# An SSM convolution with a ReLU MLP: the filter loaded in two halves, its tables made in another order and on other engines

## The chip, the core and the metric

The kernel runs on one core of a Trainium2 chip. The core has a matrix engine (TensorE, "PE" in the profile, with its weight loads as "PEld"), a vector engine (VectorE, "DVE"), a scalar engine (ScalarE, "ACT"), a general engine (GpSimd, "POOL") and a queue engine (SyncE, "SP") that here only issues DMA transfers. ACT issues a few as well. Each engine works through its own list in order. Matmuls write to PSUM, and ACT or DVE copy the result to SBUF ("evacuate" it). POOL does not touch PSUM here.

The metric is the time of one execution on the device in microseconds (us), the median over runs.

## The reference

Sequence length S is 2048, width D is 512, the hidden width of the MLP is 1376. All inputs are bf16.

```python
def A(q, k, v, shift_k, ssm_k, ssm_D):
    k_shift = sum over t < 4 of k_pad[:, t:t+S] * shift_k[:, 3 - t]   # short causal filter
    kv = k_shift * v
    y = causal convolution of kv with ssm_k over the places (FFT of length 2S, cut to S)
    y = y + kv * ssm_D
    return q * y

def B(x, w1, w2):
    return relu(x @ w1) @ w2

h   = x + A(layernorm(x), k, v, shift_k, ssm_k, ssm_D)      # x is A_q
out = h + B(layernorm(h), w1, w2)
```

## The kernel before, in words

The long convolution is a transform of length 4096 in two stages, done as matmuls against tables of sines that the kernel makes itself. The order of work is written out by hand: the framework keeps the order of the calls per engine and adds the waits. What sets the order around the change is therefore the list of calls at the end of the function (L476 to L556).

**Tables.** `_turns` (L182) makes whole-number phases on DVE with two operations, a multiply-add and a bitwise mask; `_sin` (L177) turns them into sines on ACT. The first stage's table is `f1f` (128 x 64). It is split into a bf16 high and low part (`f1hi`, `f1lo`, L242 to L244), and `paired` (L253) spreads the two over `f1w` with one memset and eight POOL copies of 32 partitions each. The second stage's table is `tab` (128 x 32 x 4 x 64): slots 0 and 1 come from ACT in four pieces (`sines2`, L272), slots 2 and 3 are their negatives, made by POOL (`negated`, L275). The phases of the pieces with i = 1 are put in two buffers (`tb`, L138) that belong to `kT` before k is loaded there. `inverse_turns` (L291) prepares phases of the inverse tables on POOL.

**Loads.** `load_rows` (L104) brings ssm_k into `kfl`, eight transfers of 256 KB: row groups 0 and 2 on SP's queue, 1 and 3 on ACT's. `wsh` (shift_k) and `drow` (ssm_D) are small transfers on ACT's queue. Then SP's queue brings k, transposed, in four chunks (`load_k`, L140), v in six transfers (`load_v`, L112), the first quarter of x (`load_x0`, L161, into `qn0`), and w1 in four (`load_w1`, L154).

**Stages.** `warm` (L418) issues matmuls whose result is not used. `s1(0)` to `s1(7)` are the first stage for ssm_k (`stage1`, L343; matmuls L350 for ssm_D's term, `drow2`, and L358). Each writes two PSUM tiles, and a string such as "AD" says which engine evacuates which (A is ACT, D is DVE). s1(gb) uses the places 8 gb to 8 gb + 7 of `kfl`. `tap(u, eng)` (L368) is the short filter over k as matmuls against `wdiag`, which `diagonals` (L261) makes on POOL from `wsh`. `second_k(kp, eng)` (L396) is the second stage for ssm_k, 16 calls, each needing slots 0 to 2 of its part of `tab`. `row(q)` (L466, L329) transposes the filtered k and multiplies by v on DVE into `xfl`, the input called "x" of the convolution. Then eight `stage1` calls do x's first stage into `a1x`, 16 `product` calls (L571) do its second stage and the products with the filter's transform, and the inverse follows (L612 on), with the gating, both layer norms and the MLP.

In the products DVE multiplies the one half from PSUM (L580); the other half (L585) is multiplied by POOL for ten of the 16, from an SBUF copy that ACT makes (L579, three buffers), and by DVE for the rest.

PSUM has four tiles (two pools of two, `bank2`, L322), taken in turn. So a matmul group may have to wait until the group four tiles earlier has been evacuated.

**x's layer norm and w1.** `bn_stats`, `moments` (L444) and `norm_rows` (L451) normalise the first quarter of x in place in `qn0`, on DVE but for two small POOL operations. `column_means` (L404) sums w1 over its rows with matmuls, and `center` (L412) subtracts the means from w1 on POOL.

Of the kernel before, what the change touches and what calls it, by code (L numbers as in the profile page):

```python
# [15 lines left out]
P = 128  # L16
# [39 lines left out]
def kernel(  # L56
# [47 lines left out]
    def load_rows(eng, rg):  # L104
        for d in range(2):
            src = bass.AP(tensor=A_ssm_k.tensor, offset=A_ssm_k.offset + S * first_channel(rg, d), ap=[[64, 32], [S, 64], [1, 64]])
            eng.dma_start(out=kfl[32 * rg:32 * rg + 32, :, d, :], in_=src)
# [4 lines left out]
    def load_v(r):  # L112
        for d in range(2) if r % 2 else (0,):
            n = 64 if r % 2 else P
            src = bass.AP(tensor=A_v.tensor, offset=A_v.offset + first_channel(r, d), ap=[[64 * D, 32], [D, 64], [1, n]])
            nc.sync.dma_start(out=vfl[32 * r:32 * r + 32, :, 64 * d:64 * d + n], in_=src)
# [8 lines left out]
    nc.vector.memset(drow2[:], 0.0)  # L125
    nc.scalar.dma_start(out=wsh[:], in_=A_shift_k.rearrange("(r p) j -> p r j", p=P))
    nc.scalar.dma_start(out=drow[0:P:16, :], in_=A_ssm_D.rearrange("(r g) -> r g", g=64))
    load_rows(nc.scalar, 1)
    for rg in (0, 2):
        load_rows(nc.sync, rg)  # L130
# [5 lines left out]


    tb = [chunk(f"tb{b}")[:].rearrange("p c t -> p (c t)").bitcast(I32)[:, 0:1024].rearrange("p (a b) -> p a b", b=64) for b in range(2)]  # L138
# [83 lines left out]
    load_rows(nc.scalar, 3)  # L222
# [5 lines left out]

    def turns2(i, b):
        ta = tb[b] if i else early.tile([P, 16, 64], I32, tag="ta", name="ta", bufs=2)[:]  # L230
        _turns(ta, r2, n2c[:], 8192, o2[:, i, b:b + 1])
        return ta

    ta00 = turns2(0, 0)
    ta01 = turns2(0, 1)
    f1hi = consts.tile([P, 64], BF16, name="f1hi")
    f1lo = consts.tile([P, 64], BF16, name="f1lo")
    f1d = early.tile([P, 64], F32, name="f1d")


    tab = tabp.tile([P, 32, 4, 64], F32R, name="tab")
    nc.vector.tensor_copy(out=f1hi[:], in_=f1f[:])  # L242
    nc.vector.tensor_tensor(out=f1d[:], in0=f1f[:], in1=f1hi[:], op=ALU.subtract)
    nc.vector.tensor_copy(out=f1lo[:], in_=f1d[:])  # L244

    f1w = consts.tile([P, 2, 2, 64], BF16, name="f1w")

    def spikes():
        for rg in range(DC):
            q = slice(32 * rg, 32 * rg + 32)  # L250
            nc.vector.tensor_copy(out=drow2[q, rg % 2, :], in_=drow[q, :])  # L251

    def paired():  # L253
        nc.gpsimd.memset(f1w[:], 0.0)
        for rg in range(DC):
            for i, f in enumerate((f1hi, f1lo)):
                nc.gpsimd.tensor_copy(out=f1w[32 * rg:32 * rg + 32, i, rg % 2, :], in_=f[32 * rg:32 * rg + 32, :])  # L257
# [14 lines left out]
    def sines2(i, b, ta):  # L272
        _sin(tab[:, 16 * i:16 * i + 16, b, :], ta, 8192)

    def negated(i):  # L275
        nc.gpsimd.tensor_single_scalar(out=tab[:, 8 * i:8 * i + 8, 2:4, :], in_=tab[:, 8 * i:8 * i + 8, 0:2, :].bitcast(F32),
                                       scalar=-1.0, op=ALU.mult)
# [173 lines left out]
    def norm_rows(q, out, src):  # L451
        for i in range(4):
            t = 4 * q + i
            nc.vector.tensor_scalar(out=out[:, i, :], in0=src[:, i, :], scalar1=mv1[:, t, 0:1],
                                    scalar2=rstd1[:, t, :], op0=ALU.subtract, op1=ALU.mult)
# [19 lines left out]

    load_k(0)  # L476
    load_k(1)
    spikes()
    sines2(0, 0, ta00)
    ta10 = turns2(1, 0)  # L480
    sines2(0, 1, ta01)
    ta11 = turns2(1, 1)
    diagonals()
    paired()
    negated(0)
    negated(1)
    sines2(1, 0, ta10)
    sines2(1, 1, ta11)
    load_k(2)
    load_k(3)  # L490
    load_v(0)
    load_v(2)
    load_x0()
    load_v(1)
    load_v(3)
    load_w1()
    negated(2)
    negated(3)
    inverse_turns()
    warm(13, lhsT=wdiag[:, 0, 0:2].rearrange("p j g -> p (j g)"))  # L500
# [3 lines left out]
    tap(0, "A")  # L504
    s1(3, "AD")
    s1(4, "AD")
    tap(1, "D")
    s1(5, "AD")
    s1(6, "AD")
    s1(7, "AD")  # L510
    tap(2, "A")
    second_k(0, "A")
    second_k(1, "D")
    second_k(2, "A")
    tap(3, "A")
    second_k(3, "D")
    second_k(4, "A")
    tap(4, "A")
    second_k(5, "D")
    pairs_pool()  # L520
    second_k(6, "A")
    tap(5, "D")
    nc.vector.bn_stats(out=st[:, 0, :], in_=qn0[:, 0, :])
    second_k(7, "A")
    tap(6, "A")
    nc.vector.bn_stats(out=st[:, 1, :], in_=qn0[:, 1, :])
    second_k(8, "A")
    tap(7, "D")
    nc.vector.bn_stats(out=st[:, 2, :], in_=qn0[:, 2, :])
    nc.vector.bn_stats(out=st[:, 3, :], in_=qn0[:, 3, :])  # L530
    moments(mv1, rstd1, 0)
    second_k(9, "A")
    row(0)
    second_k(10, "D")
    norm_rows(0, qn0, qn0)
    second_k(11, "A")
    row(1)
    second_k(12, "A")
    row(2)
    second_k(13, "D")  # L540
    second_k(14, "A")
    row(3)
    second_k(15, "A")
    pl.pop("front")
    a1xp = pl.push("a1xp")
    a1x = a1xp.tile([P, 2, 32, 256], F32R, name="a1x")
    for gb in range(8):
        stage1(lambda g: xfl[:, g // 4, :, :, g % 4], a1x, gb, ("DA", "AD", "AD", "AD", "AA", "AD", "AD", "AD")[gb])
        if gb == 0:
            column_means(0)  # L550
            for n in (0, 1):
                center(n)
        if gb == 2:
            column_means(1)
            for n in (2, 3):
                center(n)  # L556
    pl.pop("xp", "rows")

    late = pl.push("late")
    prod = pl.push("prod")  # L560
# [295 lines left out]
```

## Time and profile before

| | |
|---|---|
| three runs | 203.06, 203.39, 203.69 us; median 203.39 |
| the profiled execution | 203.05 us, of which the span (first to last instruction) is 201.3 us |
| busy in the span | PE 172.1, PEld 109.2, DVE 147.5, ACT 98.0, POOL 90.7 us |
| moved | 15.99 MB in 51,379 packets |
| chain that ended last | PE 67%, DVE 18%, POOL 4%, ACT 4% |

A row of the profile names a source line (L358 is line 358 of the kernel above), an engine, an operation, and `output<-inputs` by the program's names, with partitions x elements. "ACTq" and "SPq" are the issuing of DMA transfers by those engines; such a row's length is the time of the issue, not of the transfer, and the time to landing counts from the start of the issue. In a timeline row the first number is the start in us from the beginning of the span, the second the length; "x31" says that 31 neighbouring instructions are merged, and the bracket at the end gives the idle time before and what ended it. In a group row the numbers after the bar are busy us, mean ns of one, idle us before them and who ended it. In a list of waits the numbers are us in total, times, and the longest.

### The profile page before, as it was taken

What the parts mean: (1) busy time and instruction counts of PE and PEld (TensorE: products, weight loads), DVE (VectorE), ACT (ScalarE), POOL (GpSimd) and SP (SyncE); (2) the same over time, 40 slices, a digit from 0 to 9 for tenths busy, and PEclk for the clock granted to TensorE, in tenths of its full rate; (3) what the DMA queues carried; (4) which work ended last, traced back from release to release, by engine and by line L of the source; (5) the groups of instructions that cost most, each with busy time, mean ns of one, the idle gap of its engine ahead of it and who ended that gap; (6) DMA issues with size and microseconds to landing.
All of it is one profiled execution on the core that took longest, in us unless ns stands there. A gap on an engine that the chain in (4) does not pass through costs nothing.

```text
span 201.3 us, 4078 instructions
## 1 busy us (share of the span) xinstructions
PE 172.1 (86%) x1638; PEld 109.2 (54%) x1643; DVE 147.5 (73%) x259; ACT 98.0 (49%) x112; POOL 90.7 (45%) x108
## 2 busy tenths in 40 slices
PE   0369989899896877778967999999999999999992
PEld 0127866498775666656745654545454444444451
DVE  7957866999557999999999779979977580471142
ACT  0387688924786566522985568102630174026300
POOL 7999983120299699991985720220130011002000
PEclk9999999999999999999999999999999999999999
DMA  8999999960000000005902540312420272120022
GB/s 118 216 233 200 212 205 145 187 146 0 3 3 3 0 5 0 0 3 160 235 22 52 154 129 11 61 37 61 101 47 19 61 83 50 38 54 13 3 54 52
DMA packets 51379, 15.99 MB, mean 79 GB/s; under 512 B 46784, under 2 KB 50208, under 8 KB 51360
## 3 DMA queue, kind: packets, MB, share of 16 engines
q1 hardware_dynamic: 42464, 14.61, 35.8%
q10 hardware_dynamic: 8896, 1.12, 3.6%
q8 instruction: 13, 0.21, 0.4%
q14 instruction: 6, 0.05, 0.1%
HBM read 9.64 MB, written 2.10 MB: 58 GB/s over the span
## 4 chain that ended last, share of the span: by engine, by line
PE 67%; DVE 18%; POOL 4%; ACT 4%; issue 3%; ACTq 2%; DVEq 0%; POOLq 0%
PE m L726 19%; PE m L781 18%; DVE a1x L580 7%; PE ps L358 5%; DVE zs L619 5%; PE ps2k L388 4%; PE u L388 4%; PE pkv L375 3%; PE pst L333 3%; DVE a1k L585 3%; ACT a1x L317 3%; PE pz L646 3%; PE pi L614 2%; PE pz L656 2%; POOL f1w L257 2%
## 5 line engine op out<-in xcount | busy, mean ns | idle before, releaser
L762 ACT ACTIVATE h1T<-m 128x512 bf16<-128x512 f32 (+1 forms) x44 | 25.9, 598 | 43.5 <-PE m L726 43.5
L726 PE MATMUL m<-hT,w 128*128 128x512 bf16 (+1 forms) x176 | 39.0, 379 | 0.2 <-ACT hT L693 0.2
L781 PE MATMUL m<-w,h1T 128*128 128x512 bf16 (+1 forms) x161 | 36.1, 379 | 0.2
L787 DVE SCALAR_TENSOR_TENSOR o<-m,rstd,hp 128x128 bf16<-128x128 f32 (+1 forms) x48 | 15.8, 388 | 25.7 <-PE m L781 24.9
L448 POOL TENSOR_SCALAR rstd<-mv 128x4 f32<-128x4 f32 x8 | 1.8, 231 | 64.4 <-DVE mv L446 64.4
L726 PEld LDWEIGHTS <-w 128*128 128x128 bf16 (+1 forms) x176 | 17.4, 100 | 20.4 <-issue 0.5
L781 PEld LDWEIGHTS <-h1T 128*128 128x128 bf16 (+1 forms) x165 | 16.0, 98 | 19.3 <-issue 0.3
L388 PE MATMUL u<-a1x,tab 64*128 64x256 f32 x256 | 19.7, 291 | 6.4 <-DVE a1k L585 2.4
L585 POOL TENSOR_TENSOR a1k<-usb,a1k 128x1024 fp32r<-128x1024 f32 x10 | 23.7, 2393 | 2.3 <-DVE a1x L580 2.2
L627 ACT CAST a1x<-zs 128x1024 fp32r<-128x1024 f32 (+2 forms) x10 | 17.3, 1730 | 11.1 <-DVE zs L619 11.1
L388 PEld LDWEIGHTS u<-a1x,tab 64*128 64x128 f32 x256 | 16.4, 185 | 9.7 <-DVE a1x L580 4.2
L580 DVE TENSOR_TENSOR a1x<-u,a1k 128x1024 fp32r<-128x1024 f32 x16 | 19.1, 1218 | 2.2 <-PE u L388 2.2
L625 POOL CAST a1x<-zs 128x1024 fp32r<-128x1024 f32 (+1 forms) x8 | 15.7, 1969 | 7.4 <-DVE zs L619 7.4
L619 DVE STREAM_TRANSPOSE zs<-pi 128x1024 f32<-128x1024 f32 x16 | 18.4, 1215 | 0.5 <-PE pi L614 0.5
L414 POOL TENSOR_TENSOR w<-w,wm 128x1376 bf16<-128x1376 bf16 x4 | 11.2, 2844 | 11.3 <-ACT wm L410 11.3
L614 PE MATMUL pi<-a1k,wd 128*128 128x512 f32 x32 | 13.3, 417 | 2.6 <-DVE zs L619 1.5
L579 ACT COPY usb<-u 128x1024 f32<-128x1024 f32 x10 | 10.1, 1016 | 10.3 <-PE u L388 10.3
L317 ACT CAST a1k<-ps2k 128x1024 fp32r<-128x1024 f32 x11 | 11.0, 1027 | 7.1 <-PE ps2k L388 7.0
L614 PE MATMUL pi<-a1x,wd 128*128 128x512 f32 x32 | 12.8, 400 | 0.0
L319 DVE CAST a1k<-ps 128x1024 fp32r<-128x1024 f32 x8 | 9.6, 1222 | 4.4 <-PE ps L358 4.4
L319 DVE CAST a1x<-ps 128x1024 fp32r<-128x1024 f32 x7 | 8.4, 1222 | 5.1 <-PE ps L358 5.1
L421 PE MATMUL warm<-zero,wdiag 128*128 128x512 bf16 x13 | 4.5, 518 | 8.4 <-DVE drow L251 8.4
(116 smaller groups left out, 281.1 us busy)
## 6 DMA issues: line engine op xcount, KB each, us to landing
xall<-in_A_q_dram SPq DMA_DIRECT2D x16, 128.0 KB, 3.3
out_dram<-o SPq DMA_DIRECT2D x62, 32.0 KB, 1.6
w<-in_B_w_dram SPq DMA_DIRECT2D x4, 344.0 KB, 6.1
w<-in_B_w_dram SPq DMA_DIRECT2D x1, 1280.0 KB, 7.7
kfl<-in_A_ssm_k_dram SPq DMA_DIRECT2D x4, 256.0 KB, 5.6
kfl<-in_A_ssm_k_dram ACTq DMA_DIRECT2D x4, 256.0 KB, 6.7
vfl<-in_A_v_dram SPq DMA_DIRECT2D x2, 512.0 KB, 6.7
vfl<-in_A_v_dram SPq DMA_DIRECT2D x4, 256.0 KB, 5.4
```

The lines of the kernel that those rows point to most:

```text
L317: nc.scalar.copy(out=o, in_=i)
L319: nc.vector.tensor_copy(out=o, in_=i)
L388: nc.tensor.matmul(out=ps[:, d, 256 * i:256 * i + 256], lhsT=tab[rw, k1, b:b + 2, :].rearrange("p b k -> p (b k)"), rhs=a_in[rw, c, k1, :] ...
L580: nc.vector.tensor_tensor(out=spot(a1x, kp), in0=u2[:], in1=kk.bitcast(F32), op=ALU.mult)
L585: (nc.gpsimd if pool else nc.vector).tensor_tensor(out=kk, in0=(usb if pool else u1)[:], in1=kk.bitcast(F32), op=ALU.mult)
L614: nc.tensor.matmul(out=ps[:, b, :], lhsT=wd[:, m:m + 2, :].rearrange("p b k -> p (b k)"), rhs=src[:, d, 16 * b:16 * b + 16, c0:c0 + 32], s ...
L619: nc.vector.transpose(out=zs[:], in_=ps[:].rearrange("p b (k c) -> p c (b k)", c=32))
L627: nc.scalar.copy(out=o, in_=i)
L726: nc.tensor.matmul(out=ps1[:fsz].rearrange("p (i t) -> p i t", i=4), lhsT=w1[:, c, fc * P:fc * P + fsz], rhs=hT[sc][:, c // 2, :, c % 2, : ...
L762: nc.scalar.activation(out=h1T[:fsz, fc, :], in_=ps1[:fsz], func=ACT.Relu)
L781: nc.tensor.matmul(out=ps2[:], lhsT=lhsT, rhs=w2[:ksz, fc, :], start=(fc == 0), stop=(fc == NFC - 1))
L787: nc.vector.scalar_tensor_tensor(out=of(o[:], d)[:, a], in0=ps[:, a], scalar=rstd2[:, t, :], in1=pair(hp[sc][:, d, i, :])[:, a], op0=ALU.m ...
```

## The change

- **ssm_k in halves.** `load_rows(part, pairs)` loads places 0 to 31 of each channel block or places 32 to 63, so there are 16 transfers of 128 KB. The first eight come ahead of everything else on both queues. Of the second eight, ACT issues two after the sines of `f1f` and two after the first piece of `tab`. `drow` and `wsh` move to SP's queue, between the halves.
- **f1w by masks.** `paired` and `spikes` become two plus two and two DVE operations on all 128 partitions, with a 0/1 column per row group. The POOL copies, the memset and the split into `f1hi` and `f1lo` go.
- **Second table.** The phases sit in one tile `tt` of two pieces instead of in `kT`'s buffers. DVE makes the pieces with i = 0 early; the multiply-add of i = 1 goes to POOL and its mask to DVE, late, between the taps. `negated` takes one slot at a time, so there are eight of half the size, of which `negated(0, 0)` and `negated(1, 0)` come first.
- **Order.** 24 warm-up matmuls that read only `zero`, instead of 13 that need `wdiag`. All eight s1 come ahead of the first tap. The rows come later among the second_k calls. k, v, x0 and w1 are loaded in the order k, v, x0, w1.
- **w1's means.** `column_means(0)` and its `center` calls move ahead of x's first stage, `column_means(1)` from after its third to after its second call. The layer norm statistics of x's first quarter move behind the rows, and `norm_rows(0)` to POOL.

Second_k and tap evacuations are dealt out anew between ACT and DVE. The diff, with blank lines and unchanged context cut:

```diff
...
     kfl = front.tile([P, 64, 2, 64], BF16, name="kfl")
-    def load_rows(eng, rg):
-        for d in range(2):
-            src = bass.AP(tensor=A_ssm_k.tensor, offset=A_ssm_k.offset + S * first_channel(rg, d), ap=[[64, 32], [S, 64], [1, 64]])
-            eng.dma_start(out=kfl[32 * rg:32 * rg + 32, :, d, :], in_=src)
+    def load_rows(part, pairs=(0, 1)):
+        for pair in pairs:
+            for d in range(2):
+                for eng, rg in ((nc.sync, 2 * pair), (nc.scalar, 2 * pair + 1)):
+                    src = bass.AP(tensor=A_ssm_k.tensor, offset=A_ssm_k.offset + S * (first_channel(rg, d) + 32 * part),
+                                  ap=[[64, 32], [S, 32], [1, 64]])
+                    eng.dma_start(out=kfl[32 * rg:32 * rg + 32, 32 * part:32 * part + 32, d, :], in_=src)
     vfl = front.tile([P, 64, P], BF16, name="vfl")
-    def load_v(r):
-        for d in range(2) if r % 2 else (0,):
-            n = 64 if r % 2 else P
-            src = bass.AP(tensor=A_v.tensor, offset=A_v.offset + first_channel(r, d), ap=[[64 * D, 32], [D, 64], [1, n]])
-            nc.sync.dma_start(out=vfl[32 * r:32 * r + 32, :, 64 * d:64 * d + n], in_=src)
+    def load_v(eng, r, d):
+        n = 64 if r % 2 else P
+        src = bass.AP(tensor=A_v.tensor, offset=A_v.offset + first_channel(r, d), ap=[[64 * D, 32], [D, 64], [1, n]])
+        eng.dma_start(out=vfl[32 * r:32 * r + 32, :, 64 * d:64 * d + n], in_=src)
     zero = consts.tile([P, 512], BF16, name="zero")
     nc.vector.memset(zero[:], 0.0)
...
     nc.vector.memset(drow[:], 0.0)
     drow2 = consts.tile([P, 2, 64], BF16, name="drow2")
-    nc.vector.memset(drow2[:], 0.0)
-    nc.scalar.dma_start(out=wsh[:], in_=A_shift_k.rearrange("(r p) j -> p r j", p=P))
-    nc.scalar.dma_start(out=drow[0:P:16, :], in_=A_ssm_D.rearrange("(r g) -> r g", g=64))
-    load_rows(nc.scalar, 1)
-    for rg in (0, 2):
-        load_rows(nc.sync, rg)
+    load_rows(0)
+    nc.sync.dma_start(out=drow[0:P:16, :], in_=A_ssm_D.rearrange("(r g) -> r g", g=64))
+    nc.sync.dma_start(out=wsh[:], in_=A_shift_k.rearrange("(r p) j -> p r j", p=P))
     CH = 512
...
         return front.tile([P, DC, CH + 16], BF16, tag="kT", name=name, bufs=4)
-    tb = [chunk(f"tb{b}")[:].rearrange("p c t -> p (c t)").bitcast(I32)[:, 0:1024].rearrange("p (a b) -> p a b", b=64) for b in range(2)]
     def load_k(c):
         kT[c] = chunk("kT")
...
     f1f = early.tile([P, 64], F32, name="f1f")
     _sin(f1f[:, 0:32], t1[:, 0:32], 128)
     _sin(f1f[:, 32:64], t1[:, 32:64], 128, neg=True)
-    load_rows(nc.scalar, 3)
+    load_rows(1, (0,))
     o2 = consts.tile([P, 2, 2], F32, name="o2")
...
                                     op0=ALU.mult, op1=ALU.add)
+    tab = tabp.tile([P, 32, 4, 64], F32R, name="tab")
+    tt = early.tile([P, 2, 16, 64], I32, name="tt")
     def turns2(i, b):
-        ta = tb[b] if i else early.tile([P, 16, 64], I32, tag="ta", name="ta", bufs=2)[:]
-        _turns(ta, r2, n2c[:], 8192, o2[:, i, b:b + 1])
-        return ta
-    ta00 = turns2(0, 0)
-    ta01 = turns2(0, 1)
-    f1hi = consts.tile([P, 64], BF16, name="f1hi")
-    f1lo = consts.tile([P, 64], BF16, name="f1lo")
-    f1d = early.tile([P, 64], F32, name="f1d")
-    tab = tabp.tile([P, 32, 4, 64], F32R, name="tab")
-    nc.vector.tensor_copy(out=f1hi[:], in_=f1f[:])
-    nc.vector.tensor_tensor(out=f1d[:], in0=f1f[:], in1=f1hi[:], op=ALU.subtract)
-    nc.vector.tensor_copy(out=f1lo[:], in_=f1d[:])
+        t = tt[:, b]
+        (nc.gpsimd if i else nc.vector).tensor_scalar(out=t, in0=r2, scalar1=n2c[:], scalar2=o2[:, i, b:b + 1],
+                                                      op0=ALU.mult, op1=ALU.add)
+        if not i:
+            masked(b)
+    def masked(b):
+        nc.vector.tensor_single_scalar(out=tt[:, b], in_=tt[:, b], scalar=8191, op=ALU.bitwise_and)
+    mask = consts.tile([P, 2], F32, name="mask")
+    nc.vector.memset(mask[:], 0.0)
+    for rg in range(DC):
+        nc.vector.memset(mask[32 * rg:32 * rg + 32, rg % 2:rg % 2 + 1], 1.0)
     f1w = consts.tile([P, 2, 2, 64], BF16, name="f1w")
+    def paired():
+        for r in range(2):
+            nc.vector.tensor_scalar(out=f1w[:, 0, r, :], in0=f1f[:], scalar1=mask[:, r:r + 1], scalar2=None, op0=ALU.mult)
+        for r in range(2):
+            nc.vector.scalar_tensor_tensor(out=f1w[:, 1, r, :], in0=f1f[:], scalar=mask[:, r:r + 1], in1=f1w[:, 0, r, :],
+                                           op0=ALU.mult, op1=ALU.subtract)
     def spikes():
-        for rg in range(DC):
-            q = slice(32 * rg, 32 * rg + 32)
-            nc.vector.tensor_copy(out=drow2[q, rg % 2, :], in_=drow[q, :])
-    def paired():
-        nc.gpsimd.memset(f1w[:], 0.0)
-        for rg in range(DC):
-            for i, f in enumerate((f1hi, f1lo)):
-                nc.gpsimd.tensor_copy(out=f1w[32 * rg:32 * rg + 32, i, rg % 2, :], in_=f[32 * rg:32 * rg + 32, :])
+        for r in range(2):
+            nc.vector.tensor_scalar(out=drow2[:, r, :], in0=drow[:], scalar1=mask[:, r:r + 1], scalar2=None, op0=ALU.mult)
     wdiag = rows.tile([P, DC, KS, 64], BF16, name="wdiag")
...
     wm = rows.tile([P, 4, 344], F32, name="wm")
-    def sines2(i, b, ta):
-        _sin(tab[:, 16 * i:16 * i + 16, b, :], ta, 8192)
-    def negated(i):
-        nc.gpsimd.tensor_single_scalar(out=tab[:, 8 * i:8 * i + 8, 2:4, :], in_=tab[:, 8 * i:8 * i + 8, 0:2, :].bitcast(F32),
+    def sines2(i, b):
+        _sin(tab[:, 16 * i:16 * i + 16, b, :], tt[:, b], 8192)
+    def negated(i, b):
+        nc.gpsimd.tensor_single_scalar(out=tab[:, 8 * i:8 * i + 8, 2 + b, :], in_=tab[:, 8 * i:8 * i + 8, b, :].bitcast(F32),
                                        scalar=-1.0, op=ALU.mult)
...
         nc.gpsimd.tensor_single_scalar(out=r[:, ts, :], in_=mv[:, ts, 1:2], scalar=EPS, op=ALU.add)
         nc.gpsimd.tensor_tensor(out=r[:, ts, :], in0=r[:, ts, :], in1=mhalf[:, 0:4].unsqueeze(2), op=ALU.pow)
-    def norm_rows(q, out, src):
+    def norm_rows(q, out, src, eng=nc.vector):
         for i in range(4):
             t = 4 * q + i
-            nc.vector.tensor_scalar(out=out[:, i, :], in0=src[:, i, :], scalar1=mv1[:, t, 0:1],
+            eng.tensor_scalar(out=out[:, i, :], in0=src[:, i, :], scalar1=mv1[:, t, 0:1],
                                     scalar2=rstd1[:, t, :], op0=ALU.subtract, op1=ALU.mult)
     xfl = None
...
         for kp, eng in zip(kps, engs):
             second_k(kp, eng)
+    turns2(0, 0)
+    paired()
+    turns2(0, 1)
+    spikes()
+    sines2(0, 0)
+    load_rows(1, (1,))
     load_k(0)
     load_k(1)
-    spikes()
-    sines2(0, 0, ta00)
-    ta10 = turns2(1, 0)
-    sines2(0, 1, ta01)
-    ta11 = turns2(1, 1)
-    diagonals()
-    paired()
-    negated(0)
-    negated(1)
-    sines2(1, 0, ta10)
-    sines2(1, 1, ta11)
     load_k(2)
     load_k(3)
-    load_v(0)
-    load_v(2)
+    load_v(nc.sync, 0, 0)
+    load_v(nc.sync, 2, 0)
+    load_v(nc.sync, 1, 0)
+    load_v(nc.sync, 1, 1)
+    load_v(nc.sync, 3, 0)
+    load_v(nc.sync, 3, 1)
     load_x0()
-    load_v(1)
-    load_v(3)
     load_w1()
-    negated(2)
-    negated(3)
-    inverse_turns()
-    warm(13, lhsT=wdiag[:, 0, 0:2].rearrange("p j g -> p (j g)"))
+    diagonals()
+    warm(24)
     s1(0, "AD")
     s1(1, "AD")
     s1(2, "AD")
-    tap(0, "A")
+    inverse_turns()
+    negated(0, 0)
+    negated(1, 0)
     s1(3, "AD")
     s1(4, "AD")
-    tap(1, "D")
     s1(5, "AD")
     s1(6, "AD")
-    s1(7, "AD")
-    tap(2, "A")
+    sines2(0, 1)
+    turns2(1, 0)
+    turns2(1, 1)
+    s1(7, "DA")
+    tap(0, "A")
+    tap(1, "D")
+    masked(0)
     second_k(0, "A")
-    second_k(1, "D")
+    tap(2, "D")
+    masked(1)
+    sines2(1, 0)
+    second_k(1, "A")
+    tap(3, "D")
+    sines2(1, 1)
+    negated(2, 0)
+    negated(3, 0)
+    negated(0, 1)
+    negated(1, 1)
+    negated(2, 1)
+    negated(3, 1)
     second_k(2, "A")
-    tap(3, "A")
     second_k(3, "D")
     second_k(4, "A")
-    tap(4, "A")
-    second_k(5, "D")
+    tap(4, "D")
+    second_k(5, "A")
     pairs_pool()
     second_k(6, "A")
-    tap(5, "D")
+    second_k(7, "D")
+    tap(5, "A")
+    second_k(8, "A")
+    second_k(9, "D")
+    tap(6, "A")
+    second_k(10, "D")
+    tap(7, "A")
+    second_k(11, "D")
+    second_k(12, "A")
+    row(0)
+    second_k(13, "A")
+    row(1)
+    second_k(14, "A")
+    row(2)
     nc.vector.bn_stats(out=st[:, 0, :], in_=qn0[:, 0, :])
-    second_k(7, "A")
-    tap(6, "A")
-    nc.vector.bn_stats(out=st[:, 1, :], in_=qn0[:, 1, :])
-    second_k(8, "A")
-    tap(7, "D")
-    nc.vector.bn_stats(out=st[:, 2, :], in_=qn0[:, 2, :])
-    nc.vector.bn_stats(out=st[:, 3, :], in_=qn0[:, 3, :])
-    moments(mv1, rstd1, 0)
-    second_k(9, "A")
-    row(0)
-    second_k(10, "D")
-    norm_rows(0, qn0, qn0)
-    second_k(11, "A")
-    row(1)
-    second_k(12, "A")
-    row(2)
-    second_k(13, "D")
-    second_k(14, "A")
     row(3)
     second_k(15, "A")
+    column_means(0)
+    for n in (0, 1):
+        center(n)
+    nc.vector.bn_stats(out=st[:, 1, :], in_=qn0[:, 1, :])
+    nc.vector.bn_stats(out=st[:, 2, :], in_=qn0[:, 2, :])
     pl.pop("front")
...
         if gb == 0:
-            column_means(0)
-            for n in (0, 1):
-                center(n)
-        if gb == 2:
+            nc.vector.bn_stats(out=st[:, 3, :], in_=qn0[:, 3, :])
+            moments(mv1, rstd1, 0)
+        if gb == 1:
             column_means(1)
             for n in (2, 3):
                 center(n)
+        if gb == 2:
+            norm_rows(0, qn0, qn0, nc.gpsimd)
     pl.pop("xp", "rows")
     late = pl.push("late")
```

## The prediction

> **What bounds the kernel now.** I read the page's slices first, then TensorE's timeline of the first 65 us, then who waits for whom there, then the start of the DMA queues, last the groups of POOL.
>
> ```profile
> PE   0369989899896877778967999999999999999992
> DMA  8999999960000000005902540312420272120022
> ```
>
> One digit is 5.03 us. TensorE (PE) is idle or half idle for three slices and busy from there on, so the path is: wait for the first stage's inputs, then PE work with few gaps. The DMA engines are busy for eight slices, to about 44 us: whatever is pulled forward has to find its data there.
>
> ```profile
> 8.43 4.47 PE L421 MATMUL warm<-zero,wdiag 128*128 128x512 bf16 x13 [8.43 <-DVE drow L251]
> 13.06 0.22 PE L358 MATMUL ps<-f1w,kfl 64*128 64x128 bf16 x1
> 14.90 1.05 PE L358 MATMUL ps<-f1w,kfl 64*128 64x128 bf16 x31 [1.62 <-issue]
> ```
>
> Columns: start, length, engine, line. The first stage of ssm_k (L358) starts in earnest at 14.90. Two things end just before: POOL's last copy into f1w (L257, 13.86), and the last ssm_k transfer, issued on ACT's queue at 7.78 and landing 7.0 later, at 14.8.
>
> ```profile
> 7.78 2.41 ACTq L107 DMA_DIRECT2D kfl<-in_A_ssm_k_dram  x1
> 7.70 1.85 DVE L251 COPY drow<-drow 32x64 bf16<-32x64 bf16 x4
> 13.63 0.23 POOL L257 COPY f1w<-f1lo 32x64 bf16<-32x64 bf16 x1
> ```
>
> Later marks of the same timeline: second_k(0) starts at 28.46 (after eight s1 and three taps), x's first stage at 50.99, the products at 64.39, the inverse at 92.4. Between 28.46 and 50.99 PE waits little:
>
> ```profile
> PE pst L333 <- DVE ksh L319: 0.8, 1, 0.8
> PE ps L358 <- DVE xfl L335: 0.8, 1, 0.8
> PE ps2k L388 <- DVE a1k L319: 0.6, 1, 0.6
> ```
>
> From 92.4 on nothing is changed and the chain is PE work nearly throughout, so a shift at the inverse is a shift of the end.
>
> **The change, step by step.**
>
> *Start of s1(0).* It needs half of ssm_k, f1w and drow2. Half the transfers: before, four of the eight 256 KB transfers had landed by 8.05 (SP's three issues at 0.72, 1.19 and 2.25, landing 3.1, 5.3 and 5.8 later, ACT's at 2.41, landing 4.4 later). Eight of 128 KB on two queues from 0.72 are the same bytes: about 7.6. f1f: ACT issues four half transfers instead of wsh, drow and two whole ones (to 5.02), so its table load and the two sines (1.83 us together) end near 5.3 to 6.9. DVE: o2 ends at 3.95; five small memsets at 0.1 (the spacing of L170) reach 4.45; turns2(0,0) 1.45 (L184 and L185, 3.88 to 5.33), 5.9; four 64-wide operations for f1w at 0.19 to 0.34 (L242 to L244), 0.25 taken, 6.9; turns2(0,1) 1.45, or 2.06 where POOL works beside it (the tb rows, 1.29 and 0.77), 8.4 to 9.0; two for drow2 at 0.13 to 0.57 (L251, whose long ones ran beside POOL's wdiag, as these may), 8.7 to 10.1. I take **10.2** with PE's start: 4.7 earlier. The nine POOL operations of f1w (10.02 to 13.86) go. The 24 warm-ups need only zero (written at 1.1): seven started 0.427 apart in the row above, the rest at about 0.22, so 1.2 to about 8.0.
>
> *Eight s1.* From 14.90 to 28.46 are eight s1 and three taps of 0.99: 1.32 per s1, evacuation included. s1(4) would start at 10.2 + 4 x 1.32 = 15.5 and needs the second half. ACT issues its part between f1f, sines2(0,0) and the first evacuation; the rate so far (one 256 KB per 1.25 to 1.35 us) puts the last landing at 12.3, the old lag (7.0 from issue) on an issue at 9 puts it at 16. Nothing is charged to it at 13 to 15. Two taps come ahead of second_k(0) instead of three, so it starts at 10.2 + 10.6 + 2.0 = 22.8, like for like 23.8 against 28.46: **-4.7**.
>
> *Tables.* In time order: sines2(0,1) follows s1(6)'s evacuation on ACT (about 20); POOL does wdiag to 11, inverse_turns 7.0 (24.91 to 31.92), two negations of half of L276 (1.39), 20.8; turns2(1,b) at L307's 1.20 each, the second behind sines2(0,1), to 23; DVE's two masks 0.69 each stand behind taps 1 and 2, with tap 2's and 3's evacuation queued behind them; ACT's two late sines (1.12 each) stand ahead of the evacuations of second_k(1) and (2), and PE waits there if all four PSUM tiles are full. ACT was busy 14.35 of 22.50 us in 28.5 to 51, so this is mostly hidden: **+0.4**; without that room the 2.2 us of sines would show.
>
> *To x's first stage.* Tap 7 now has two second_k between it and row(0), so the 0.75 before pst goes, and column_means(0) (1.27) stands where PE waited 0.80 for xfl: **-1.5**. PE would be ready for w1's means at 50.99 - 4.7 - 1.5 + 0.4 = 45.2. But w1 has to be there:
>
> ```profile
> 37.80 0.60 SPq L159 DMA_DIRECT2D w<-in_B_w_dram  x1
> ```
>
> It landed 7.1 later, at 44.9, the last of the stream. The bytes are the same; SP's queue takes over drow and wsh (1.14 and 0.48 of issue), and x0 moves behind v without a change of sum. I take 45.4: **+0.2**. Bounds: 43.5 and, by the 1.6 in full and more, 47.
>
> *x's first stage.* 13.40 before (50.99 to 64.39) with two means in it. With one, PE has 1.27 less, but ACT and DVE evacuate 1.02 and 1.22 per tile, and two tiles and one means fewer does not take the full 1.27 out: I take 12.6, so **+0.5** for the means now paid ahead of it (0 to 1.0).
>
> *norm_rows on POOL.* The four DVE operations (0.41 each) go to POOL, behind the four subtractions of w1 and ahead of the products' POOL half.
>
> ```profile
> L585 POOL TENSOR_TENSOR a1k<-usb,a1k 128x1024 fp32r<-128x1024 f32 x10 | 23.7, 2393 | 2.3 <-DVE a1x L580 2.2
> L414 POOL TENSOR_TENSOR w<-w,wm 128x1376 bf16<-128x1376 bf16 x4 | 11.2, 2844 | 11.3 <-ACT wm L410 11.3
> L276 POOL TENSOR_SCALAR tab<-tab 128x1024 fp32r<-128x1024 f32 x4 | 11.0, 2776 | 0.1
> L307 POOL TENSOR_SCALAR rf<-rf,k1o,ofc 128x1024 int32<-128x1024 int32 x1 | 1.2, 1202 | 0.1
> ```
>
> POOL is what the products lean on: ten of 2.39 in 28 us, idle 2.3 of them, 1.6 of that before the first. From x's start, POOL's stream is 0.9 (means copied) + 11.4 (L414) + 1.3 (L448, L449) + 4p = 13.6 + 4p; the first product wants POOL at 16.1 before, 15.3 now. So POOL is late by 4p - 1.7. Free are 0.9 (its last product ended at 91.46, PE was released by DVE at 92.33) and the 0.65 of gaps between. No row has bf16 with two column scalars: 512 elements cost 0.60 by L307 (two scalars, int32), 1.06 by L414's rate (bf16), 1.39 by L276 (one scalar, f32). I take 1.06, the row with its type: 2.5 late, **+1.0**; the ends are 0 and +2.3.
>
> The Trainium skill (GPSIMD Engine Reference, 3.1) measures 769 ns for 512 elements in a tight loop with one input; by it POOL would be 1.4 late, inside the free part, and the sum 1.0 lower. No run here shows that price.
>
> **Sum:** -4.7 + 0.4 - 1.5 + 0.2 + 0.5 + 1.0 = -4.1. The profiled execution took 203.05 (span 201.3 and 1.75 around it): 198.95. It is the lowest of the runs shown but for 0.01 (203.06 to 203.69, median 203.39); I say **199.0**.
>
> **Rivals.**
>
> *The early front is carried whole.* drow2 at 8.7, w1 at 43.5 and POOL at 0.60: 1.3 more from the front, 1.0 from POOL, 0.2 from w1: 196.5. For it: three of the prices were taken near the dear end. Against: w1 was the last to land and the queue is no shorter.
>
> *POOL or the stream eats more.* POOL at 1.39 is +1.3 on the forecast, w1 at 47 is +1.6: 200.3 to 201.9.
>
> *The halves bring nothing sooner.* The DMA slices are 9s, so splitting could only reorder. The Trainium skill (Perfetto Trace Analysis, DMA Optimizations) says splitting may let the whole task end sooner if DMA engines are generally idle; here they are not, and the trace agrees that the stream as a whole will not end sooner. As a mechanism: the second half lands at 18 instead of by 15.5, and s1(4) to s1(7) wait 2.5: 201.5.
>
> *PE goes slow again between warm-ups and s1(0).* The first seven warm-ups ran at half the pace of the rest; a gap of 1.62 before 14.90 did not bring that back (31 matmuls in 1.05). Now the gap is 8.0 to 10.2. If drow2 is later than about 11.4, s1(0) and s1(1) could run at half pace, 1.1 more each, on top of 1.2 later: 202. The Trainium skill (TensorE: Matmul & The Clock Gate, Why this matters for your kernels) puts the limit at gaps of about 3 us. By that rule 2.2 is safe.
>
> *Slower: the SP queue.* Ahead of k's first transpose SP now issues ten transfers instead of four, each waiting, in the program as built, for the landing of the transfer eight issues back over both queues. k's transposes, v, x0 and w1 all queue behind, and column_means(0) now holds PE until w1 is there. PE's products start at w1's landing + 1.27 + 12.6, plus 1.0 of POOL; that passes 64.39 when w1 lands after 49.5, 4.6 later than before. If each of the six added issues costs 0.9 unhidden, w1 lands at 50.3 and the kernel takes 203.9. Against: before, a queue's next issue ended 1.5 to 2.5 ahead of the previous landing, so lags overlapped.
>
> **How the numbers follow.** Forecast 0.50 (198 to 200.2); front whole 0.17; POOL or stream 0.14; second half late 0.07; slow clock 0.03; SP queue 0.06; no change from a mixture of these 0.03. The range leaves a tenth out on each side: 196.4 to 201.9. A measurement of this kernel can tell about 0.3% (0.6 us) from no change: faster 0.90, same 0.03, slower 0.07.
>
> **What would show it.** L358 of ssm_k starting at 10.2 (8.9 to 11); no PE wait at s1(4); column_means(0) starting at w1's landing near 45; norm_rows on POOL at 1.06 each and the first POOL product 2 to 3 us after ACT's copy. A start of s1(0) after 12, a wait of over 2 us before s1(4), or means starting after 48 would make it wrong.

## The result: slower by 4.4%

The changed kernel takes 212.69 us (210.98 to 213.31, four runs) against 203.54 (203.06 to 203.74) for the kernel before on the same chip: ratio 1.044, interval 1.037 to 1.051. The forecast was 199.0. The profiled execution took 213.31, span 211.5. (The profiled executions of e5, e8, e10 and e11 are slow ones, 2 to 4 us above their medians, so only rates and marks of the front are read from these, and ratios leave slow executions out.) A single time below is a median in us; differences between kernels are differences of their ratios to the kernel before, times 203.5.

The page's slices of the changed kernel, one digit 5.29 us, as read before the change but with the granted clock and the rate:

```profile
PE   7598999964896766774897799999999999999992
PEclk9969999978599999999599999999999999999999
DMA  8999999997000000000690261220350225121012
GB/s 110 141 144 147 192 190 150 149 203 159 0 3 3 2 3 0 0 3 0 170 225 2 50 207 62 50 53 22 73 107 0 54 49 99 25 50 25 3 47 54
```

TensorE begins early, as forecast, but the stream of loads now ends at 53 us, not 44, and with the DMA engines just as busy it moves 141 to 147 GB/s in the second to fourth slices. Before:

```profile
GB/s 118 216 233 200 212 205 145 187 146 0 3 3 3 0 5 0 0 3 160 235 22 52 154 129 11 61 37 61 101 47 19 61 83 50 38 54 13 3 54 52
```

TensorE's timeline, its clock by stretches (columns from "us" to "POOL": busy time and instructions of each engine; then clock, DMA busy share, GB/s), and the groups of POOL, all of the changed kernel:

```profile
10.72 0.40 PE L351 MATMUL ps<-drow,ind 64*128 64x256 bf16 x4 [2.62 <-DVE kT L140]
10.95 2.09 PE L359 MATMUL ps<-f1w,kfl 64*128 64x128 bf16 x32
...
45.41 3.57 PE L334 MATMUL pst<-ident,ksh 128*128 128x128 bf16 x32 [1.65 <-DVE xfl L336]
...
53.79 1.90 PE L409 MATMUL pm<-w,ones 128*128 128x344 bf16 x6 [3.17 <-DMA w<-in_B_w_dram]
...
69.42 2.12 PE L389 MATMUL u<-a1x,tab 64*128 64x256 f32 x32 [1.55 <-ACT a1x L318]
...
80.93 1.68 PE L389 MATMUL u<-a1x,tab 64*128 64x256 f32 x24 [2.16 <-ACT usb L592]
...
101.15 0.80 PE L627 MATMUL pi<-a1k,wd 128*128 128x512 f32 x1 [3.25 <-POOL a1k L598]
```

```profile
11.00:15.00 4.00, 3.98 (x76) 3.86 (x75) 1.23 (x1) 1.04 (x2) 3.63 (x16) 0.57 1.58 143
...
54.00:59.00 5.00, 5.00 (x70) 3.94 (x68) 1.39 (x2) 1.75 (x2) 2.46 (x1) 0.50 0.00 0
```

```profile
L598 POOL TENSOR_TENSOR a1k<-usb,a1k 128x1024 fp32r<-128x1024 f32 x10 | 23.7, 2430 | 0.0
...
L455 POOL TENSOR_SCALAR qn<-qn,mv,rstd 128x512 bf16<-128x512 bf16 x4 | 8.2, 2065 | 0.0
```

Three losses stand here, as shifts in the profiled executions. w1's last transfer landed at 53.74 (before 44.9), and the means waited for it: the products begin at 69.42 instead of 64.39, +5.0. norm_rows takes 2.07 each on POOL, whose ten products then have no idle time before them, and the inverse waits 3.25 for the last: from the products' start to the inverse's second half it is 31.73 instead of 27.98, +3.8. The matmuls behind that wait run at half clock, and from the inverse's second half to the end it is 1.4 longer; the three make up the 10.2 between the spans. Four times in all the granted clock fell to about half behind a wait: after those of 2.62, 3.17 and 3.25, and after the 1.65 at 45.41 (0.54 from 46 to 49 us), where `xfl` was held up by a late v. Behind the 2.16 at 80.93 it stayed whole.

### The profile page after: what moved, and what is told of

It is laid out like the page before. It is cut to its first block, busy times and chain, and to the rows that moved or that the text cites. A ratio compares the mean times of both kernels' runs of the same rounds, so it can differ in the third digit from the quotient of the medians.

```text
span 211.5 us, 4112 instructions
## 1 busy us (share of the span) xinstructions
PE 181.7 (86%) x1654; PEld 116.1 (55%) x1654; DVE 145.0 (69%) x257; ACT 96.6 (46%) x111; POOL 98.4 (47%) x109
## 3 DMA queue, kind: packets, MB, share of 16 engines
q10 hardware_dynamic: 8416, 1.11, 5.8%
## 4 chain that ended last, share of the span: by engine, by line
PE 52%; SPq 15%; DMA 9%; DVE 9%; POOL 6%; issue 3%; ACT 3%; ACTq 0%; DVEq 0%; POOLq 0%
PE m L739 18%; PE m L794 17%; SPq L119 6%; DMA kfl<-in_A_ssm_k_dram 5%; PE pi L627 5%; DVE a1x L593 4%; DMA w<-in_B_w_dram 4%; SPq L143 4%; POOL a1k L598 3%; PE ps L359 3%; DVE zs L632 3%; SPq L141 3%; PE pz L659 2%; ACT a1x L318 2%; PE u L389 2%
## 5 line engine op out<-in xcount | busy, mean ns | idle before, releaser
L739 PEld LDWEIGHTS <-w 128*128 128x128 bf16 (+1 forms) x176 | 17.3, 100 | 20.5 <-issue 0.5
L389 PEld LDWEIGHTS u<-a1x,tab 64*128 64x128 f32 x256 | 16.3, 184 | 11.6 <-ACT usb L592 4.8
L627 PE MATMUL pi<-a1k,wd 128*128 128x512 f32 x32 | 14.8, 462 | 4.8 <-POOL a1k L598 3.3
L627 PE MATMUL pi<-a1x,wd 128*128 128x512 f32 x32 | 14.1, 442 | 0.0
L277 POOL TENSOR_SCALAR tab<-tab 128x512 fp32r<-128x512 f32 x8 | 12.7, 1609 | 2.9 <-ACT tab L176 2.9
```

What stands on the lines that cost most here:

```text
L389: nc.tensor.matmul(out=ps[:, d, 256 * i:256 * i + 256], lhsT=tab[rw, k1, b:b + 2, :].rearrange("p b k -> p (b k)"), rhs=a_in[rw, c, k1, :] ...
L627: nc.tensor.matmul(out=ps[:, b, :], lhsT=wd[:, m:m + 2, :].rearrange("p b k -> p (b k)"), rhs=src[:, d, 16 * b:16 * b + 16, c0:c0 + 32], s ...
L739: nc.tensor.matmul(out=ps1[:fsz].rearrange("p (i t) -> p i t", i=4), lhsT=w1[:, c, fc * P:fc * P + fsz], rhs=hT[sc][:, c // 2, :, c % 2, : ...
```

## The experiments

What made the loads slow was not seen at first, and the first two sets looked for it in the wrong place.

**First set: issues and places in the order of calls.** All four keep the changed kernel's tiles.

*e1_small_first*: `wsh` and `drow` first, on ACT's queue.

```diff
-    load_rows(0)
-    nc.sync.dma_start(out=drow...)
-    nc.sync.dma_start(out=wsh...)
+    nc.scalar.dma_start(out=wsh...)
+    nc.scalar.dma_start(out=drow...)
+    load_rows(0)
```

> The changed kernel with ssm_D's and shift_k's two small transfers put back ahead of everything on ACT's queue; all else as changed. Theory A (the two small transfers between the halves, and the rule that a transfer waits for the landing of the one eight issues back, hold SP's queue): k's first transpose is issued at 9 or before instead of 11.9, drow2 and wdiag come earlier, w1 lands at 45 to 48 instead of 53.7, x's products start 5 to 7 us earlier than 69.4, and the kernel takes 205.5 to 208.5. Rival B (transfers of 128 KB move the bytes at a lower rate in themselves): w1 still lands after 50 and the kernel takes 209.5 or more.

212.02, ratio 1.042 (1.038 to 1.045). The rate stays (first slices 110, 142, 144, 153 GB/s) and w1 lands 52.79. The small transfers are not the cause.

*e2_norm_dve*: `norm_rows(0, qn0, qn0, nc.gpsimd)` without its last argument. *e3_small_dve*: e1 and e2 together.

> The changed kernel with norm_rows of x's first quarter on DVE again, at the same place in the order. Theory: the four POOL operations of 2.06 us each hold POOL's first product until 77.4 and its last until 101.1, so PE stands 3.25 us before the inverse and runs its first matmuls there at half pace. With them gone POOL's first product starts by 73, PE waits less than 0.5 us for POOL at the inverse, TensorE's granted clock stays whole there, and the kernel takes 207.0 to 209.0 (3.8 us of wait and 1.4 of slow matmuls less). Rival (DVE, now with four more operations of 0.41, or w1's lateness sets the end anyway): 210.5 or more.

> Both of the two edits before together: small transfers first on ACT's queue, norm_rows on DVE. If A and the POOL theory hold and are independent, their gains add: 201 to 203.5. If B holds, it is as the kernel with norm_rows on DVE alone, 207 or more.

e2 215.78, ratio 1.059 (1.054 to 1.063); e3 215.48, 1.058 (1.053 to 1.062): worse still. The group of e2:

```profile
L455 DVE TENSOR_SCALAR qn<-qn,mv,rstd 128x512 bf16<-128x512 bf16 x4 | 6.3, 1645 | 1.1 <-POOL rstd L450 1.1
```

At this place POOL runs the centers beside it, and the four take 1.65 each instead of 0.41; the evacuations behind them on DVE hold PE for 7.5 in x's first stage. But from the products' start to the inverse it is 28.0 again: POOL's 3.8 is gone. The norm is dear here on either engine.

*e4_means_back*: the means behind x's first and third call, as before the change.

> The changed kernel with column_means(0) and its subtractions behind x's first call and column_means(1) behind its third, as before the change; w1 still lands late. Theory A: PE is no longer held with nothing done, but the means still wait for w1 near 53.7 right after the first call: products start 1.5 to 2.5 us earlier than 69.4, POOL's stream (subtractions, then norm_rows) starts no earlier, so little of it reaches the end: 210 to 212.5. Rival C (it is the place of the means alone that costs, and the late w1 would be hidden): 207 or less.

211.84, ratio 1.041 (1.037 to 1.045). The products begin 3.2 earlier (66.19), but ACT then waits 11.6 for POOL to free `usb`, so 1.4 of it reaches the end of the span (0.7 by the ratios, which is inside their intervals). The two losses lie partly behind each other.

**Second set: parts put into, or taken out of, the two kernels.**

*e5_whole*: the changed kernel with the kernel before's `load_rows`, queue order and warm-up.

> The changed kernel with ssm_k loaded as before the change: eight whole transfers, shift_k and D first on ACT's queue, rg 1 and then (behind f1f) rg 3 on ACT's queue, rg 0 and 2 on SP's, and before's warm-up of 13 on wdiag; the order of the compute, the tables, v's order and x's norm on POOL stay changed. Theory B (the 128 KB halves themselves slow the stream of loads): k's first transpose is issued at 6 to 7 us instead of 11.89, the slice at 5 to 10 us is back above 200 GB/s, the last of w1 has landed by 47 instead of 53.74, the products begin at 63.5 to 66 instead of 69.42, and what is left over the kernel before is POOL's norm (about 3.8): 205.5 to 208.5. Rival V (the order in which v and x0 are asked for, or anything else than the halves, holds the stream): w1 lands at 51 or later, and the time is 210 to 213.

214.66, ratio 1.054 (1.050 to 1.059). Whole transfers are slow there too (146, 168, 178 GB/s in the second to fourth slices). Theory B fell here, and even more in the next.

*e6_halves_alone*: the kernel before with halves.

```diff
-    load_rows(nc.scalar, 1)
-    for rg in (0, 2):
-        load_rows(nc.sync, rg)
+    load_rows(0)
...
-    load_rows(nc.scalar, 3)
+    load_rows(1)
```

> The kernel before with only ssm_k's load cut in halves: sixteen transfers of 128 KB in the changed kernel's order on both queues, shift_k and D still first on ACT's queue, everything else as before the change. Theory B: the rate falls to 110 to 150 GB/s while the halves are moved, k's first transpose is issued at 10.5 or later instead of 6.57, w1 lands at 50 or later instead of 44.9, and the time grows to 206 to 210. Rival V (the halves are not to blame): k's transposes and w1 within 1.5 us of before, and 202.5 to 204.5.

202.55, ratio 0.996 (0.993 to 0.998): 0.9 faster, little but clear of noise, with 214, 240 and 197 GB/s in the same slices. So 128 KB transfers are not slow in themselves.

*e7_norm_alone*: the kernel before with `norm_rows(0)` on POOL behind its fourth center.

> The kernel before with only the four norm_rows of x's first four blocks moved: from DVE ahead of the rows to POOL behind its third and fourth center, as in the changed kernel. Theory A (POOL's share of the products is on the path, and 8.2 us are put ahead of it): the four take 8.0 to 8.5 us, POOL's ten products end 3 to 4.5 us later, the inverse waits for them, and the time is 206.5 to 208.5. Rival (POOL has slack enough when the products start as early as before, and the price in the changed kernel came from elsewhere): 203 to 205.

209.00, ratio 1.029 (1.027 to 1.031): **+5.9** for four instructions. The waits of its products and inverse, and its clock (one digit 5.19 us; the two 6s lie in the products, behind the wait of 3.3, and at the inverse):

```profile
ACT usb L579 <- POOL a1k L585: 10.3, 7, 5.6
...
PE u L388 <- ACT usb L579: 3.3, 1, 3.3
```

```profile
PEclk9999999999999996999699999999999999999999
```

The products begin at 64.56 as before (64.39), and the inverse's second half waits 2.12 for POOL and starts at 97.19, 4.7 late by the 27.98 above. From 98.24 on eight matmuls run at 0.60 to 0.63 each instead of 0.40, and start 0.43 apart instead of 0.24: 1.5 more, the rest of the loss.

*e8_whole_early*: e5, with x0 back between v's parts, statistics and norm back on DVE ahead of the rows, and the means back.

> The kernel of whole transfers (tables by masks, turns of the second table on POOL, the changed order of taps and second products), and beside that x0 back between v's parts, the statistics and the norm of x's first blocks back ahead of the rows and on DVE, and the means of w1 back behind x's first and third call. What is left of the change is the tables and the order of ssm_k's stages. If the three moved parts (halves, norm on POOL, means ahead) carry the whole loss, this one is at 202 to 204.5 (the tables alone were put at +0.4 in the prediction). If the changed tables or the order cost something of their own, it is above 205; if they gain without the halves, below 202.

208.97, ratio 1.026 (1.022 to 1.030). All three suspects are out, and 5.4 us of loss are still there. Its loads are those of the kernel before, in the same order, and still move only 155, 156 and 180 GB/s in the second to fourth slices, so what slows them is in none of the loading code. Besides the making of the tables and the order of ssm_k's stages, what e5 and e8 share with the changed kernel, and e6 doesn't, is the list of tiles.

**Third set: the place of the tiles.** The pools give tiles their addresses in the order of the program, each rounded up to 32 B. Among the constants, the change takes out `f1hi` and `f1lo` (128 B of each partition apiece) and puts in `mask` (8 B, rounded to 32): 224 B less in all. w1's, ssm_k's, v's and k's tiles come after the constants, so they all move. In the built programs `kfl` begins at byte 40,192 of the partition before the change (157 x 256) and at 39,968 after it, 32 past a multiple of 128. ssm_k is written in rows of 128 B.

*e9_pad*: the changed kernel, one size changed, no instruction added.

```diff
-    mask = consts.tile([P, 2], F32, name="mask")
-    nc.vector.memset(mask[:], 0.0)
+    mask = consts.tile([P, 64], F32, name="mask")
+    nc.vector.memset(mask[:, 0:2], 0.0)
```

> The changed kernel with one size changed and no instruction: the tile mask is 128x64 instead of 128x2 (its first two columns are used as before), so that the constants take as many bytes as in the kernel before and every tile behind them lies where it lay before the change. In the built programs ssm_k's tile begins at byte 40192 of each partition before the change (a multiple of 256), at 39968 after it (32 past a multiple of 64), here at 40192 again. Theory P (place: rows of 128 B written 32 B off their 64 B boundary are slow): the first four slices are back at 200 GB/s and above, k's first transpose is issued at 8 or earlier instead of 11.89, the last of w1 has landed by 48 instead of 53.74, s1 runs at whole pace, the products begin at 62 to 65.5 instead of 69.42; the norm on POOL (+5.8 alone) and the means stay: 203.5 to 208. Rival Q (something in the changed program's order slows the loads, the tables or the turns on POOL): GB/s stay at 110 to 150 and the time at 211 to 213.

205.00, ratio 1.008 (1.004 to 1.012): **-7.4** for a wider tile. Its slices (5.09 us each) and its timeline:

```profile
GB/s 128 203 169 159 218 222 131 231 186 1 3 3 2 3 0 0 3 0 100 241 72 51 89 192 0 52 56 58 95 55 14 64 75 57 32 58 13 3 52 53
```

```profile
8.71 0.40 PE L351 MATMUL ps<-drow,ind 64*128 64x256 bf16 x4 [0.26 <-DVE kT L140]
8.93 1.28 PE L359 MATMUL ps<-f1w,kfl 64*128 64x128 bf16 x32
...
46.63 1.90 PE L409 MATMUL pm<-w,ones 128*128 128x344 bf16 x6 [2.28 <-DMA w<-in_B_w_dram]
...
61.66 2.14 PE L389 MATMUL u<-a1x,tab 64*128 64x256 f32 x32 [1.55 <-ACT a1x L318]
```

The first s1 takes 1.28 instead of 2.09, the means get w1 7.2 earlier, the products begin at 61.66 instead of 69.42. Three of theory P's marks were missed: of the first four slices only the second is above 200, the third and fourth stay at 169 and 159, k's first transpose was issued at 9.63 (before the change 6.57), not by 8, and the products begin 0.3 ahead of the range given.

*e10_shift32*, *e11_shift64*, *e13_shift128*: the kernel before with its last constant, `mhalf`, 128 x 16, 24 or 40 instead of 128 x 4. The instructions are the same ones in the same order.

> The kernel before with one size changed and no instruction: the last constant, mhalf, is 128x16 instead of 128x4 (four columns used as before), so that w1, ssm_k's, v's and k's tiles begin 32 B further on: ssm_k's at 40224 instead of 40192. Theory P: the rate of the first slices falls to 110 to 170 GB/s at a DMA share of 9, w1 lands 6 to 10 us later than 44.9, and the time grows to 206 to 212 with the same instructions. Rival Q: within 0.5 of the kernel before.

> As the run with 32 B, with mhalf 128x24: the tiles behind it begin 64 B further on than before, ssm_k's at 40256. If it is the 64 B boundary that counts, nothing changes: within 0.7 of the kernel before. If 128 B or 256 B count (a row of 128 B then lies across such a boundary), the loads are slowed here too: over 205.

> The kernel before with mhalf 128x40, no instruction changed: the tiles behind it begin 128 B further on, ssm_k's at 40320 (a multiple of 128, not of 256). If the 128 B rows only have to begin at a multiple of 128, nothing changes: within 0.7 of the kernel before, first slices above 200 GB/s. If the tile's start has to be a multiple of 256 (v's even rows are 256 B long and now lie across such a boundary), or if any displacement is slow, over 205.

210.34, ratio 1.034 (1.030 to 1.038); 210.74, 1.035 (1.027 to 1.042); 203.95, 1.002 (0.999 to 1.004). So 32 or 64 B of displacement cost **7 us** in the kernel before, with nothing else changed, and 128 B nothing. The row of ACT's DMA queue (packets, MB, time of its packets as a share of sixteen engines' span), which moves half of ssm_k and little else until the last stores; the kernel before, then displaced by 32, 64 and 128 B:

```profile
q10 hardware_dynamic: 8896, 1.12, 3.6%
```

```profile
q10 hardware_dynamic: 8896, 1.12, 5.6%
```

```profile
q10 hardware_dynamic: 8896, 1.12, 5.4%
```

```profile
q10 hardware_dynamic: 8896, 1.12, 3.6%
```

The same packets and bytes: 3.6% of 16 x 201.3 us over 8,896 packets is 13.0 ns a packet (a packet is here, nearly always, one row of 128 B), then 21.2, 20.5 and 13.1 with their spans (210.9, 210.7, 202.3). In the changed kernel it is 23.3 (5.8%, 8,416 packets), in e9 13.9.

**Fourth set: the parts with the tiles in place.** *e12_pad_early* is e9 with e8's three parts put back (x0, norm on DVE early, means behind). *e14_pad_means* is e12 with the means ahead, as in the change. *e15_pad_whole* is e12 with the kernel before's whole transfers, warm-up and place of the two small transfers. The diff shows e12 against e9, cut:

```diff
-    load_v(nc.sync, 1, 0) ... load_v(nc.sync, 3, 1)
-    load_x0()
+    load_x0()
+    load_v(nc.sync, 1, 0) ... load_v(nc.sync, 3, 1)
...
     row(0)
+    norm_rows(0, qn0, qn0)
...
-        if gb == 2:
-            norm_rows(0, qn0, qn0, nc.gpsimd)
```

> The changed kernel with mask at 128x64, and beside that x0 back between v's parts, the statistics and the norm of x's first blocks back on DVE ahead of the rows, and w1's means back behind x's first and third call. Halves, tables by masks, turns on POOL and the changed order of ssm_k's stages stay. If the prediction's front was right once the tiles lie as before (first s1 at about 10, second_k(0) 3 to 5 us earlier, no slow clock), 197.5 to 201. If halves bring nothing sooner or the order costs what it gains: 201.5 to 204.

> The run e12 (197.86) with one part of the change put back: w1's first means and its two centers ahead of x's first stage, the second ones behind x's second call. By the prediction's terms (w1 landed +0.2, means paid ahead +0.5) 198 to 199. If the wait for w1 is what it was in the changed kernel (3.7 us of PE in that trace, 2.3 in the padded one), 200 to 202.

> The run e12 (197.86) with ssm_k loaded as before the change: eight whole transfers, shift_k and D first on ACT's queue, warm-up of 13 on wdiag. By the prediction (first s1 at 10.2 instead of 14.9, of which second_k(0) keeps 4.7) 201.5 to 203.5. If the halves alone gave little (0.6 in the kernel before) and the gain is the order's and the tables', 198 to 199.5.

e12 takes **197.86**, ratio 0.970 (0.967 to 0.973): the best of all, and faster than both kernels. Its timeline and clock:

```profile
9.22 1.06 PE L359 MATMUL ps<-f1w,kfl 64*128 64x128 bf16 x32
...
21.66 0.91 PE L389 MATMUL ps2k<-a1k,tab 64*128 64x256 f32 x8
...
59.91 2.14 PE L389 MATMUL u<-a1x,tab 64*128 64x256 f32 x32 [1.54 <-ACT a1x L318]
```

```profile
PEclk9999999999999999999999999999999999999999
```

e14: 199.99, 0.980 (0.974 to 0.986). Its means wait for w1, whose last part is there at 47.9:

```profile
PE pm L409 <- DMA w<-in_B_w_dram: 1.6, 1, 1.6
```

e15: 203.51, 0.999 (0.996 to 1.003). Without the halves s1 waits for the last whole transfer until 15.30, and everything else that is left of the change is worth nothing that the interval could show.

## Why the prediction was wrong, step by step

| step | forecast | measured | from |
|---|---|---|---|
| early s1 by halves | -4.7 | -6.0 | e12 against e15 |
| tables, order of ssm_k's stages | +0.4 | -0.2 | e15 |
| w1's means ahead of x's stage | -1.5 + 0.2 + 0.5 = -0.8 | +2.0 | e14 against e12 |
| norm_rows on POOL | +1.0 | +5.7 (alone +5.9) | e9 against e14 (e7) |
| place of the tiles | not in the sum | +7.4 (alone +6.9) | changed kernel against e9 (e10) |
| sum | -4.1 | +8.9, measured +9.0 | |

The measured column has to add up: each run is the one before it with one part more, so the sum checks nothing. By the intervals each difference is good to 1 to 1.6 us.

**The step that failed first is one that wasn't there.** The ledger counted instructions, transfers and waits, and no line of it held the addresses. "The bytes are the same" and "Eight of 128 KB on two queues from 0.72 are the same bytes: about 7.6" took the old rate for granted, and the rate was lost with a tile of 8 bytes: w1, put at 45.4 for +0.2, landed at 53.7, and the place of the tiles alone is 7.4 of the 9.0. Nothing in the profile of before shows it; the list of `consts` tiles in the diff does.

The Trainium skill (SBUF — State Buffer, Operand start alignment) says that transfers into element-aligned addresses write the right bytes, and says that this is about legality, not speed. These runs add the speed. The Trainium skill (DMA: Bandwidth & Descriptors, How a descriptor splits into AXI transactions) says of reading that a transaction must start at a multiple of 256 B, and counts beats of 32 B. If the same held for writing, a pair of 128 B rows would take 4 + 8 = 12 beats in place or displaced by 128 B, 14 displaced by 32, and 16 displaced by 64: an estimate of 1.0, 1.17 and 1.33 times from that page. That 128 B costs nothing agrees; the order of 32 and 64 B and the size don't: 1.01 (128 B), 1.63 (32 B) and 1.58 (64 B) by the packets above.

**The front was right once the tiles lie as before.** Forecast were s1 at 10.2 and second_k(0) at 22.8; e12 has 9.2 and 21.7. In the changed kernel `drow`'s late landing held `drow2`, s1 began at 10.95 and ran at half pace, and second_k(0) came at 25.46. s1(4)'s wait for the second half is 0.34 in e12 and 0.88 in the changed kernel. The halves gain only together with the rest: alone (e6) they bring 0.9, because there f1w, still made by POOL, holds s1 to 14.0 anyway. The rival "the halves bring nothing sooner" falls.

**norm_rows was mis-sized.** 1.06 was taken, 1.39 given as the dear end; it is 2.07. The rows that bounded it had one property each (bf16, or two scalars, or one scalar in f32), none all three, and the dear one was half of a row twice as wide: at 128x512 the same operation takes 1.61 in the changed kernel (L277). The working around it held. With 2.07 it gives 4 x 2.07 - 1.7 = 6.6 late and, less the 0.9 and 0.65 free, +5.0; e7's inverse was 4.7 late. What it put at nothing is the half clock behind that wait, 1.5 more in e7. The Trainium skill's 769 ns (GPSIMD Engine Reference, 3.1), named beside the forecast, is for one input in a loop; the trace has 2.07 us for this form.

**The means were put where they must wait.** -1.5 was counted for two waits that would vanish. The one before `pst` did, in the changed kernel and in e9; in e12, with the statistics back ahead of the rows, PE waits 1.53 there. The other was exchanged for a wait for w1, whose landing was put at 45.4. With the tiles in place it lands at 46.6 (e9) and 47.9 (e14), just inside and past the late bound of 47, and TensorE is there for the means at 43.9 and 45.8. Why it lands later than the 44.9 of before isn't shown: in e15, where k's first transpose is issued at 6.68, as early as before, it lands at 46.5. The late landing was priced as a rival at +1.6.

**The rivals.** The one on the slower side named the right sign and mark (w1 landing after 49.5) for the wrong reason: SP's extra issues. In e9, with the same calls, w1 is there at 46.6 instead of 53.7, so 7.1 of the 8.8 us by which it came late are the place of the tiles. The slow clock was given 0.03 and came to pass, with `drow2` at 10.7 and a gap of 2.62, where the rival asked for 11.4. The length of a gap alone doesn't decide it. Half pace followed waits of 1.65, 2.62, 3.17 and 3.25 in the changed kernel, 1.63 in e1, 2.12 in e7 and 2.28 in e9; the clock stayed whole behind 1.62 in the kernel before, 1.61 in e14, 2.16 in the changed kernel and 2.40 in e3. The Trainium skill's limit of about 3 us (TensorE: Matmul & The Clock Gate, Why this matters for your kernels), behind "By that rule 2.2 is safe", isn't borne out by these traces.

**What stays open.** At 32 and 64 B every 128 B row of ssm_k lies across a multiple of 128 and every second one across a multiple of 256; at 128 B none does either. So 64 is not enough, and which of the two counts isn't told apart. All tiles behind the constants were displaced together, so ssm_k's share and v's aren't separated. And e9 against e14 moves x0 and the statistics along with the norm. Their products begin at 61.66 and 61.63, so the 5.7 arise behind that point; that the norm carries them rests on this and on e7.

## What to carry to other kernels

Before pricing a change, list the tiles that it adds, drops or resizes and see which transfers' targets move behind them: rows of 128 B written 32 B off took 21 ns a packet here instead of 13, for the whole kernel 7 us, and a wider tile mended it. If a stream slows while its bytes, packets and DMA busy share stay, look at addresses before queues. And an operation moved to another engine needs a row of its own form; where none exists, the dear end has to be wider than the neighbours.

## What the runs showed of the hardware

- Rows of 128 B written to addresses 32 or 64 B past a multiple of 128: 20.5 to 21.2 ns a packet instead of 13.0.
- TENSOR_SCALAR on POOL, 128x512 bf16 with two column scalars: 2.07 us; on DVE 0.41, but 1.65 beside POOL's TENSOR_TENSOR (e2).
- After waits of TensorE between 1.63 us (e1) and 3.25 us its granted clock often fell to half for some us: in the changed kernel 0.57 from 11 to 15 us and 0.50 from 54 to 59. After others up to 2.40 us (e3) it did not. Where it falls, a late transfer is paid twice.
